# Transposing the gate by DMA in place of TensorE, and the second matmul issued in parts

## The chip, the cores and the metric

One core of one Trainium2 chip runs the program. The metric is the device time of one execution in microseconds; the time before is the median of five runs. A core has five engines that run side by side: TensorE (PE; its weight loads are listed as PEld), VectorE (DVE), ScalarE (ACT), GpSimd (POOL) and SyncE (SP). DMA transfers are issued by POOL and SP here, each in its own order.

## The reference

```python
def _attn_ref(u, v, z):                 # u, v: (8, 3008, 256), z: (8, 3008, 64), float32
    scores = (1.0 / S) * np.matmul(z, z.transpose(0, 2, 1))      # S = 3008
    attn = np.maximum(scores, 0.0) ** 2
    out = np.matmul(attn, v)
    return u * out

def _moe_ref(x, w_in, w_out):           # w_in: (256, 2048), w_out: (2048, 256)
    h = x @ w_in
    g = h * (1.0 / (1.0 + np.exp(-1.702 * h)))
    return g @ w_out

x = _attn_ref(u, v, z).reshape(24064, 256)
result = _moe_ref(x, w_in, w_out)       # (24064, 256) float32
```

## The kernel before

The 8 batches have 3008 tokens each, cut into 6 blocks: five of 512 and one of 448, so there are 48 blocks. Everything is kept transposed: features or keys stand on the partitions, tokens of the block in the free dimension.

`attention` (L207) makes one block. For each pair of 128-key tiles TensorE makes two score tiles (L217, `sc`, from `zT` on both sides), ScalarE takes the Relu (L227, `r`), VectorE squares it (L228, `at`), and three pairs later TensorE adds the pair into two accumulators (L258, `outps`, four matmuls for a pair). At the end VectorE multiplies the accumulators by the transposed gate `uT` into `xT` (L267).

`emit_phaseB` (L153) runs in front of the next block's attention. For each of the 16 slices of the hidden width it makes `hps` (L164, two matmuls), the sigmoid on ScalarE (L172, `sig`) and the product on VectorE (L180, `g`). Between these go the matmuls of the block before that one: `emit_ygroup` (L125) sums 16 matmuls of 256 columns (L130, `yps`) for each 128 tokens, and VectorE scales the sum out (L137, `ysb`). Group 0 comes first, groups 1 and 2 after slices 5 and 10, group 3 in the attention that follows.

`uT` comes from `dma_u` (L94), which brings the block of `u` to SBUF in float32 on SP's queue, and `emit_utr` (L117): TensorE transposes each 128x128 piece in float32 against an identity (L122, `ups`) and ScalarE copies it to `uT` (L123). There are 8 such pieces in a block, and those of the next block are handed to `emit_phaseB` as `tr_jobs`. `zT` comes another way: `dma_z` (L71) casts z to float16 in flight on POOL's queue into `z_st`, whose padding VectorE zeroes (L78, L80), and `emit_ztr` (L112) transposes 24 pieces of 128x128 with one DMA on SP's queue (L113). `load_v` (L83, issued at L85) and `load_weights` (L67) are casting loads on POOL's queue.

PSUM is cut in two pools: `ps_big` has three buffers, for `sc` and `hps`; `ps_small` has two, which `outps`, `yps` and `ups` share. The tiles `uT`, `u_st`, `z_st`, `vh` and `zT` have two buffers each.

A planner fixes the order of each engine's instructions when the program is built, from the order of the program, modelled durations and the buffers that are free. It may move an instruction ahead of others of its engine, so `yps` matmuls stand between `hps` matmuls in the trace where the program has them later. What it fixed is then carried out strictly in that order on each engine.

Of the kernel before, what the change touches and what calls it, by code (L numbers as in the profile page):

```python
# [8 lines left out]

FP32 = mybir.dt.float32  # L10
FP16 = mybir.dt.float16
AF = mybir.ActivationFunctionType
ALU = mybir.AluOpType


def cdiv(a, b):
    return (a + b - 1) // b
# [3 lines left out]
def kernel(  # L21
# [9 lines left out]
    nc = tc.nc  # L31
    P = 128

    B, S, D = u.shape
    dqk = z.shape[2]
    d_ff = moe_w_in.shape[1]
    ND = D // P
# [9 lines left out]

    inv_S2 = 1.0 / (float(S) * float(S))

    const = ctx.enter_context(tc.tile_pool(name="const", bufs=1))  # L50
    wpool = ctx.enter_context(tc.tile_pool(name="wpool", bufs=1))
    zvpool = ctx.enter_context(tc.tile_pool(name="zvpool", bufs=2))
    stage = ctx.enter_context(tc.tile_pool(name="stage", bufs=2))
# [4 lines left out]
    ps_big = ctx.enter_context(tc.tile_pool(name="ps_big", bufs=3, space=bass.MemoryType.PSUM))  # L58
    ps_small = ctx.enter_context(tc.tile_pool(name="ps_small", bufs=2, space=bass.MemoryType.PSUM))

    identf = const.tile([P, P], FP32, name="identf")
    make_identity(nc, identf)

    w_inh = wpool.tile([P, ND, d_ff], FP16, name="w_inh")
    w_outh = wpool.tile([P, NF, D], FP16, name="w_outh")

    def load_weights():  # L67
        nc.gpsimd.dma_start(w_inh, moe_w_in.rearrange("(h p) f -> p h f", p=P))
        nc.gpsimd.dma_start(w_outh, moe_w_out.rearrange("(f p) d -> p f d", p=P))

    def dma_z(b):  # L71
        z_st = zvpool.tile([P, NJ, P], FP16, name=f"z_st{b}", tag="z_st")
        nc.gpsimd.dma_start(  # L73
            z_st[:, : NJ - 1, :dqk],
            z[b, : (NJ - 1) * P, :].rearrange("(n p) m -> p n m", p=P),
        )
        nc.gpsimd.dma_start(z_st[:JL, NJ - 1, :dqk], z[b, (NJ - 1) * P :, :])
        nc.vector.memset(z_st[:, :, dqk:], 0.0)  # L78
        if JL < P:
            nc.vector.memset(z_st[JL:, NJ - 1, :dqk], 0.0)  # L80
        return z_st

    def load_v(b):  # L83
        vh = zvpool.tile([P, NJ, D], FP16, name=f"vh{b}", tag="vh")
        nc.gpsimd.dma_start(  # L85
            vh[:, : NJ - 1, :],
            v[b, : (NJ - 1) * P, :].rearrange("(n p) m -> p n m", p=P),
        )
        nc.gpsimd.dma_start(vh[:JL, NJ - 1, :], v[b, (NJ - 1) * P :, :])
        if JL < P:  # L90
            nc.vector.memset(vh[JL:, NJ - 1, :], 0.0)
        return vh

    def dma_u(b, blk):  # L94
        i0, ilen = blocks[blk]
        u_st = stage.tile([P, 4, D], FP32, name=f"ust_{b}_{blk}", tag="u_st")
        fullm = ilen // P
        if fullm:
            nc.sync.dma_start(
                u_st[:, :fullm, :],  # L100
                u[b, i0 : i0 + fullm * P, :].rearrange("(n p) m -> p n m", p=P),
            )
        if ilen % P:
            nc.sync.dma_start(
                u_st[: ilen % P, fullm, :], u[b, i0 + fullm * P : i0 + ilen, :]
            )
        return u_st

    def alloc_zT(b):
        return zvpool.tile([P, SP], FP16, name=f"zT{b}", tag="zT")  # L110

# [2 lines left out]
            zT.rearrange("p (n t) -> p n t", t=P), z_st[:, :, :]  # L114
        )

    def emit_utr(b, blk, uT, u_st, idx):  # L117
        i0, ilen = blocks[blk]
        m, h = divmod(idx, ND)
        ml = min(P, ilen - m * P)  # L120
        ups = ps_small.tile([P, P], FP32, name=f"ups_{b}_{blk}_{idx}", tag="pssmall")
        nc.tensor.transpose(ups[:, :ml], u_st[:ml, m, h * P : (h + 1) * P], identf[:ml, :ml])  # L122
        nc.scalar.copy(uT[:, h, m * P : m * P + ml], ups[:, :ml])  # L123

    def emit_ygroup(pend_y, m):  # L125
        gts_y, ilen_y, tok0_y, y_sb = pend_y
        ml = min(P, ilen_y - m * P)
        yps = ps_small.tile([P, IBS], FP32, name=f"yps_{tok0_y}_{m}", tag="pssmall")
        for ff in range(NF):
            nc.tensor.matmul(  # L130
                yps[:ml, :D],
                gts_y[ff][:, m * P : m * P + ml],
                w_outh[:, ff, :],
                start=(ff == 0),
                stop=(ff == NF - 1),
            )
        nc.vector.tensor_scalar_mul(y_sb[:ml, m, :], yps[:ml, :D], inv_S2)  # L137

    def emit_ydma(pend_y):
        gts_y, ilen_y, tok0_y, y_sb = pend_y  # L140
        full = ilen_y // P
        if full:
            nc.sync.dma_start(
                out[tok0_y : tok0_y + full * P, :].rearrange("(n p) d -> p n d", p=P),
                y_sb[:, :full, :],
            )
        if ilen_y % P:
            nc.sync.dma_start(
                out[tok0_y + full * P : tok0_y + ilen_y, :],
                y_sb[: ilen_y % P, full, :],  # L150
            )

    def emit_phaseB(pend_h, pend_y, tr_jobs, full_y):  # L153
        if pend_y is not None:
            emit_ygroup(pend_y, 0)
        new_pend = None
        if pend_h is not None:
            xT, ilen, tok0 = pend_h
            y_sb = work.tile([P, 4, D], FP32, name=f"ysb_{tok0}", tag="ysb")
            gts = []  # L160
            for f in range(NF):
                hps = ps_big.tile([P, IBS], FP32, name=f"hps_{tok0}_{f}", tag="psbig")
                for h in range(ND):
                    nc.tensor.matmul(  # L164
                        hps[:, :ilen],
                        w_inh[:, h, f * P : (f + 1) * P],
                        xT[:, h, :ilen],
                        start=(h == 0),
                        stop=(h == ND - 1),
                    )  # L170
                sig = sigp.tile([P, IBS], FP16, name=f"sig_{tok0}_{f}", tag="sig")
                nc.scalar.activation(  # L172
                    out=sig[:, :ilen],
                    in_=hps[:, :ilen],
                    func=AF.Sigmoid,
                    bias=0.0,
                    scale=1.702 * inv_S2,
                )
                gt = gpool.tile([P, IBS], FP16, name=f"g_{tok0}_{f}", tag=f"g{f}")
                nc.vector.tensor_tensor(gt[:, :ilen], hps[:, :ilen], sig[:, :ilen], ALU.mult)  # L180
                gts.append(gt)
                if pend_y is not None:
                    nsub_y = cdiv(pend_y[1], P)
                    if f == 5 and nsub_y > 1:
                        emit_ygroup(pend_y, 1)
                    elif f == 10 and nsub_y > 2:
                        emit_ygroup(pend_y, 2)
                ti = f // 2
                if f % 2 == 1 and ti < len(tr_jobs):
                    tr_jobs[ti]()  # L190
            for job in tr_jobs[NF // 2 :]:
                job()
            new_pend = [gts, ilen, tok0, y_sb]
        else:
            if pend_y is not None:
                for m in range(1, cdiv(pend_y[1], P)):
                    emit_ygroup(pend_y, m)
            for job in tr_jobs:
                job()
        if pend_y is not None and full_y:  # L200
            nsub_y = cdiv(pend_y[1], P)
            if pend_h is not None and nsub_y > 3:
                emit_ygroup(pend_y, 3)
            emit_ydma(pend_y)
        return new_pend

    def attention(b, blk, zT, vh, uT, pend_y):  # L207
# [57 lines left out]
        xT = work.tile([P, ND, IBS], FP16, name=f"xT_{b}_{blk}", tag="xT")  # L265
        for h in range(ND):
            nc.vector.tensor_tensor(  # L267
                xT[:, h, :ilen], outps[h][:, :ilen], uT[:, h, :ilen], ALU.mult
            )
        return xT  # L270

# [1 line left out]
    vh_cur = load_v(0)  # L273
    zT_cur = alloc_zT(0)
    emit_ztr(zT_cur, z_st_cur)
    u_st = dma_u(0, 0)
    load_weights()
    uT = stage.tile([P, ND, IBS], FP32, name="uT_0_0", tag="uT")
    for i in range(2 * cdiv(blocks[0][1], P)):
        emit_utr(0, 0, uT, u_st, i)  # L280

    z_st_next = vh_next = zT_next = None
    pend_h = None
# [2 lines left out]
    for b in range(B):  # L286
        zT = zT_cur
        vh = vh_cur
        for blk, (i0, ilen) in enumerate(blocks):
# [1 line left out]
                z_st_next = dma_z(b + 1)  # L291
                vh_next = load_v(b + 1)
            nxt = (b, blk + 1) if blk + 1 < NBLK else (b + 1, 0)
            tr_jobs = []
            uT_next = None
            if nxt[0] < B:
                u_st_n = dma_u(*nxt)
                uT_next = stage.tile(
                    [P, ND, IBS], FP32, name=f"uT_{nxt[0]}_{nxt[1]}", tag="uT"
                )  # L300
                nsub_n = cdiv(blocks[nxt[1]][1], P)
                for i in range(2 * nsub_n):
                    tr_jobs.append(
                        (lambda i=i, a=nxt[0], c=nxt[1], t=uT_next, s=u_st_n:
                         emit_utr(a, c, t, s, i))
                    )
            if b + 1 < B and blk == 1:
                zT_next = alloc_zT(b + 1)
                emit_ztr(zT_next, z_st_next)
            new_pend = emit_phaseB(pend_h, pend_y, tr_jobs, full_y=False)  # L310
            old_pend_y = pend_y
            pend_y = new_pend
            xT = attention(b, blk, zT, vh, uT, old_pend_y)
# [1 line left out]
            uT = uT_next  # L315
        zT_cur = zT_next
        vh_cur = vh_next
    pend_y2 = emit_phaseB(pend_h, pend_y, [], full_y=True)
    emit_phaseB(None, pend_y2, [], full_y=True)


# [28 lines left out]
```

## Time and profile before

| | |
|---|---|
| median of 5 runs | 1592.23 us (1589.49 to 1596.23) |
| profiled execution, its own time | 1594.62 us |
| its span, first to last instruction | 1592.9 us |
| mean granted TensorE clock | 0.998 of full speed |
| TensorE busy | 1484.8 us, 8448 matmuls |
| VectorE busy / ScalarE busy | 1034.0 us / 1046.4 us |
| DMA | 74.49 MB |

Busy time counts an instruction from its start to its modelled end. TensorE overlaps the end of one matmul with the start of the next, so the sum of durations is more than the time that they take up; distances between starts tell that time.

### The profile page before, as it was taken

The numbers are of one execution on the slowest core, as the hardware profiler recorded it, in microseconds if no ns is written. First come the engines' busy times: TensorE is split into PE (matmuls) and PEld (weight loads), VectorE is DVE, ScalarE is ACT, GpSimd is POOL, SyncE is SP. The second block draws the span as 40 slices with busy tenths as digits, with TensorE's granted clock in tenths as the row PEclk, the third lists the DMA queues.
The fourth block names the chain that finished last, engine by engine and source line by source line (L and its number), as shares of the span: only waits on it lengthen the run. The fifth ranks groups of instructions, "written<-read, shape, count | busy, mean of one in ns | idle before, by whom it ended". The sixth has DMA issues, their size and how long they took to land.

```text
span 1592.9 us, 22055 instructions
## 1 busy us (share of the span) xinstructions
PE 1484.8 (93%) x8448; PEld 836.3 (53%) x8448; DVE 1034.0 (65%) x1752; ACT 1046.4 (66%) x1826; POOL 35.6 (2%) x40
## 2 busy tenths in 40 slices
PE   1799999999999999999999999999999999999998
PEld 0255555555555555555555555555555555555555
DVE  0466676666766666666666666666676666766676
ACT  1576667766766767576756676667666766776665
POOL 2100010000100001000010000000000000000000
PEclk9999999999999999999999999999999999999999
DMA  9900061000700016001160111311032000110001
GB/s 147 128 25 27 27 96 51 26 27 27 122 26 25 28 43 106 26 26 41 40 95 26 39 40 47 66 37 40 27 73 63 27 27 27 40 39 26 14 14 39
DMA packets 125834, 74.49 MB, mean 47 GB/s; under 512 B 51232, under 2 KB 125472, under 8 KB 125728
## 3 DMA queue, kind: packets, MB, share of 16 engines
q1 hardware_dynamic: 74752, 55.58, 12.8%
q0 software_dynamic: 50976, 17.50, 10.2%
q8 instruction: 66, 1.08, 0.3%
q14 instruction: 40, 0.33, 0.1%
HBM read 59.64 MB, written 24.64 MB: 53 GB/s over the span
## 4 chain that ended last, share of the span: by engine, by line
PE 83%; ACT 6%; DVE 6%; DMA 4%; issue 1%; POOL 0%; DVEq 0%; POOLq 0%; SPq 0%
PE outps L258 29%; PE yps L130 23%; PE sc L217 15%; PE hps L164 15%; ACT sig L172 5%; DMA zT<-z_st 4%; DVE g L180 3%; DVE xT L267 2%; ACT uT L123 1%; DVE ysb L137 1%; PE ups L122 1%; DMA z_st<-in_z_dram 0%; DVE z_st L78 0%; POOL z_st L73 0%; ACT L172 0%
## 5 line engine op out<-in xcount | busy, mean ns | idle before, releaser
L172 ACT ACTIVATE sig<-hps 128x512 f16<-128x512 f32 (+1 forms) x768 | 434.7, 593 | 351.4 <-PE hps L164 295.5
L258 PE MATMUL outps<-at,vh 128*128 128x512 f16 (+1 forms) x2304 | 559.0, 375 | 7.9 <-DVE at L228 7.9
L180 DVE TENSOR_TENSOR g<-hps,sig 128x512 f16<-128x512 f32 (+1 forms) x768 | 486.6, 676 | 121.5 <-ACT sig L172 113.3
L227 ACT ACTIVATE r<-sc 128x1024 f16<-128x1024 f32 x480 | 474.3, 1028 | 121.2 <-PE sc L217 118.5
L228 DVE TENSOR_TENSOR at<-r 128x1024 f16<-128x1024 f16 x480 | 332.3, 692 | 257.5 <-ACT r L227 257.5
L130 PE MATMUL yps<-w_outh,g 128*128 128x256 f16 (+1 forms) x3072 | 419.9, 272 | 47.7 <-DVE xT L267 26.3
L164 PE MATMUL hps<-xT,w_inh 128*128 128x512 f16 (+1 forms) x1536 | 414.3, 375 | 13.2 <-DVE g L180 12.2
L130 PEld LDWEIGHTS <-g 128*128 128x128 f16 (+1 forms) x3072 | 300.4, 98 | 190.1 <-issue 90.3
L258 PEld LDWEIGHTS <-vh 128*128 128x128 f16 x2304 | 225.7, 98 | 270.9 <-issue 10.2
L217 PE MATMUL sc<-zT 128*128 128x512 f16 (+1 forms) x1152 | 323.7, 376 | 29.1 <-DMA zT<-z_st 28.9
L164 PEld LDWEIGHTS <-w_inh 128*128 128x128 f16 x1536 | 149.3, 98 | 94.4 <-issue 30.3
L217 PEld LDWEIGHTS <-zT 128*128 128x128 f16 x1152 | 111.7, 98 | 147.6 <-DMA zT<-z_st 29.2
L123 ACT COPY uT<-ups 128x128 f32<-128x128 f32 (+1 forms) x384 | 100.8, 282 | 51.0 <-PE ups L122 51.0
L137 DVE TENSOR_SCALAR ysb<-yps 128x256 f32<-128x256 f32 x192 | 80.5, 419 | 68.3 <-PE yps L130 66.8
L267 DVE TENSOR_TENSOR xT<-outps,uT 128x512 f16<-128x512 f32 (+1 forms) x96 | 60.8, 675 | 70.9 <-PE outps L258 70.9
L122 PE MATMUL ups<-identf,ust 128*128 128x128 f32 (+1 forms) x384 | 98.5, 281 | 6.4 <-DMA ust<-in_u_dram 4.6
L231 ACT ACTIVATE r<-sc 128x448 f16<-128x448 f32 x192 | 89.3, 568 | 10.9 <-PE sc L217 10.9
L236 DVE TENSOR_TENSOR at<-r 128x448 f16<-128x448 f16 x192 | 74.6, 392 | 20.0 <-ACT r L231 13.6
L122 PEld LDWEIGHTS ups<-identf,ust 128*128 128x128 f32 (+1 forms) x384 | 54.0, 142 | 49.4 <-issue 8.3
L85 POOL DMA_DIRECT2D vh<-in_v_dram x8 | 12.1, 1508 | 1099.6 <-PE outps L258 1099.6
L78 DVE MEMSET z_st<- 128x768 uint32 x8 | 5.6, 698 | 16.2 <-DMA zT<-z_st 14.9
L73 POOL DMA_DIRECT2D z_st<-in_z_dram x8 | 12.1, 1514 | 52.2 <-DMA zT<-z_st 50.9
(14 smaller groups left out, 16.7 us busy)
## 6 DMA issues: line engine op xcount, KB each, us to landing
ust<-in_u_dram SPq DMA_DIRECT2D x40, 512.0 KB, 3.9
out_dram<-ysb SPq DMA_DIRECT2D x40, 512.0 KB, 2.9
vh<-in_v_dram POOLq DMA_DIRECT2D x8, 1472.0 KB, 12.8
ust<-in_u_dram SPq DMA_DIRECT2D x8, 384.0 KB, 3.3
out_dram<-ysb SPq DMA_DIRECT2D x8, 384.0 KB, 2.6
z_st<-in_z_dram POOLq DMA_DIRECT2D x8, 368.0 KB, 12.8
w_inh<-in_moe_w_in_dram POOLq DMA_DIRECT2D x1, 1024.0 KB, 29.6
w_outh<-in_moe_w_out_dram POOLq DMA_DIRECT2D x1, 1024.0 KB, 39.3
```

The lines of the kernel that those rows point to most:

```text
L122: nc.tensor.transpose(ups[:, :ml], u_st[:ml, m, h * P : (h + 1) * P], identf[:ml, :ml])
L123: nc.scalar.copy(uT[:, h, m * P : m * P + ml], ups[:, :ml])
L130: nc.tensor.matmul(yps[:ml, :D], gts_y[ff][:, m * P : m * P + ml], w_outh[:, ff, :], start=(ff == 0), stop=(ff == NF - 1),)
L137: nc.vector.tensor_scalar_mul(y_sb[:ml, m, :], yps[:ml, :D], inv_S2)
L164: nc.tensor.matmul(hps[:, :ilen], w_inh[:, h, f * P : (f + 1) * P], xT[:, h, :ilen], start=(h == 0), stop=(h == ND - 1),)
L172: nc.scalar.activation(out=sig[:, :ilen], in_=hps[:, :ilen], func=AF.Sigmoid, bias=0.0, scale=1.702 * inv_S2,)
L180: nc.vector.tensor_tensor(gt[:, :ilen], hps[:, :ilen], sig[:, :ilen], ALU.mult)
L217: nc.tensor.matmul(scp[:, t * IBS : t * IBS + ilen], zT[:, jt * P : (jt + 1) * P], zT[:, i0 : i0 + ilen], start=True, stop=True,)
L227: nc.scalar.activation(out=rp[:, :, :], in_=scp[:, :], func=AF.Relu)
L228: nc.vector.tensor_tensor(atp[:], rp[:], rp[:], ALU.mult)
L258: nc.tensor.matmul(outps[h][:, :ilen], vh[:, jt, h * P : (h + 1) * P], atp[:, t, :ilen], start=(jt == 0), stop=(jt == NJ - 1),)
L267: nc.vector.tensor_tensor(xT[:, h, :ilen], outps[h][:, :ilen], uT[:, h, :ilen], ALU.mult)
```

## The change

The float32 transposes of u on TensorE, their copies on ScalarE, the identity and `tr_jobs` go. `load_uT` takes their place: up to four casting loads on POOL's queue bring the block of u to SBUF as float16, and two DMA transposes on SP's queue (one for each half of the features) write `uT`, now float16. In the block of 448 tokens GpSimd zeroes the staging tile first.

`gate` writes one element of a tile on GpSimd from the first `zT`, so that the loads into that tile start only after that transpose has landed: the weights, the first u, and the second batch's z and v. The zeroing of the padding of z moves from VectorE to GpSimd from the third batch on.

`emit_ygroup` can now be emitted in parts and from another pool: group 0 uses `ps_big`, and groups 1 and 2 are spread in sixths behind slices 0 to 5 and 6 to 11.

```diff
--- before.py
+++ after.py
...
-    identf = const.tile([P, P], FP32, name="identf")
-    make_identity(nc, identf)
-
     w_inh = wpool.tile([P, ND, d_ff], FP16, name="w_inh")
     w_outh = wpool.tile([P, NF, D], FP16, name="w_outh")
 
+    zT_first = []
+
+    def gate(ap):
+        # holds the loads into a tile back until the first z transpose has landed
+        nc.gpsimd.tensor_copy(ap, zT_first[0][:1, :1])
+
     def load_weights():
+        gate(w_inh[:1, 0, :1])
+        gate(w_outh[:1, 0, :1])
         nc.gpsimd.dma_start(w_inh, moe_w_in.rearrange("(h p) f -> p h f", p=P))
         nc.gpsimd.dma_start(w_outh, moe_w_out.rearrange("(f p) d -> p f d", p=P))
 
     def dma_z(b):
         z_st = zvpool.tile([P, NJ, P], FP16, name=f"z_st{b}", tag="z_st")
+        if b == 1:
+            gate(z_st[:1, 0, :1])
         nc.gpsimd.dma_start(
             z_st[:, : NJ - 1, :dqk],
             z[b, : (NJ - 1) * P, :].rearrange("(n p) m -> p n m", p=P),
         )
         nc.gpsimd.dma_start(z_st[:JL, NJ - 1, :dqk], z[b, (NJ - 1) * P :, :])
-        nc.vector.memset(z_st[:, :, dqk:], 0.0)
+        eng = nc.vector if b < 2 else nc.gpsimd
+        eng.memset(z_st[:, :, dqk:], 0.0)
         if JL < P:
-            nc.vector.memset(z_st[JL:, NJ - 1, :dqk], 0.0)
+            eng.memset(z_st[JL:, NJ - 1, :dqk], 0.0)
         return z_st
 
     def load_v(b):
         vh = zvpool.tile([P, NJ, D], FP16, name=f"vh{b}", tag="vh")
+        if b == 1:
+            gate(vh[:1, 0, :1])
         nc.gpsimd.dma_start(
             vh[:, : NJ - 1, :],
             v[b, : (NJ - 1) * P, :].rearrange("(n p) m -> p n m", p=P),
@@ -91,21 +99,6 @@
             nc.vector.memset(vh[JL:, NJ - 1, :], 0.0)
         return vh
 
-    def dma_u(b, blk):
-        i0, ilen = blocks[blk]
-        u_st = stage.tile([P, 4, D], FP32, name=f"ust_{b}_{blk}", tag="u_st")
-        fullm = ilen // P
-        if fullm:
-            nc.sync.dma_start(
-                u_st[:, :fullm, :],
-                u[b, i0 : i0 + fullm * P, :].rearrange("(n p) m -> p n m", p=P),
-            )
-        if ilen % P:
-            nc.sync.dma_start(
-                u_st[: ilen % P, fullm, :], u[b, i0 + fullm * P : i0 + ilen, :]
-            )
-        return u_st
-
     def alloc_zT(b):
         return zvpool.tile([P, SP], FP16, name=f"zT{b}", tag="zT")
 
@@ -114,19 +107,36 @@
             zT.rearrange("p (n t) -> p n t", t=P), z_st[:, :, :]
         )
 
-    def emit_utr(b, blk, uT, u_st, idx):
+    def load_uT(b, blk):
         i0, ilen = blocks[blk]
-        m, h = divmod(idx, ND)
-        ml = min(P, ilen - m * P)
-        ups = ps_small.tile([P, P], FP32, name=f"ups_{b}_{blk}_{idx}", tag="pssmall")
-        nc.tensor.transpose(ups[:, :ml], u_st[:ml, m, h * P : (h + 1) * P], identf[:ml, :ml])
-        nc.scalar.copy(uT[:, h, m * P : m * P + ml], ups[:, :ml])
-
-    def emit_ygroup(pend_y, m):
-        gts_y, ilen_y, tok0_y, y_sb = pend_y
+        nsub = cdiv(ilen, P)
+        u_st = stage.tile([P, ND, 4, P], FP16, name=f"ust_{b}_{blk}", tag="u_st")
+        if ilen < 4 * P:
+            nc.gpsimd.memset(u_st[:, :, :, :], 0.0)
+        for m in range(nsub):
+            ml = min(P, ilen - m * P)
+            if b == 0 and blk == 0:
+                gate(u_st[:1, 0, m, :1])
+            nc.gpsimd.dma_start(
+                u_st[:ml, :, m, :],
+                u[b, i0 + m * P : i0 + m * P + ml, :].rearrange("t (h dd) -> t h dd", h=ND),
+            )
+        uT = stage.tile([P, ND, 4, P], FP16, name=f"uT_{b}_{blk}", tag="uT")
+        for h in range(ND):
+            nc.sync.dma_start_transpose(uT[:, h], u_st[:, h])
+        return uT
+
+    def emit_ygroup(pend_y, m, parts=1, part=0, pool=ps_small, tag="pssmall"):
+        gts_y, ilen_y, tok0_y, y_sb = pend_y[:4]
         ml = min(P, ilen_y - m * P)
-        yps = ps_small.tile([P, IBS], FP32, name=f"yps_{tok0_y}_{m}", tag="pssmall")
-        for ff in range(NF):
+        if part == 0:
+            yps = pool.tile([P, IBS], FP32, name=f"yps_{tok0_y}_{m}", tag=tag)
+            pend_y[4] = yps
+        else:
+            yps = pend_y[4]
+        lo = NF * part // parts
+        hi = NF * (part + 1) // parts
+        for ff in range(lo, hi):
             nc.tensor.matmul(
                 yps[:ml, :D],
                 gts_y[ff][:, m * P : m * P + ml],
@@ -134,10 +144,11 @@
                 start=(ff == 0),
                 stop=(ff == NF - 1),
             )
-        nc.vector.tensor_scalar_mul(y_sb[:ml, m, :], yps[:ml, :D], inv_S2)
+        if hi == NF:
+            nc.vector.tensor_scalar_mul(y_sb[:ml, m, :], yps[:ml, :D], inv_S2)
 
     def emit_ydma(pend_y):
-        gts_y, ilen_y, tok0_y, y_sb = pend_y
+        gts_y, ilen_y, tok0_y, y_sb = pend_y[:4]
         full = ilen_y // P
         if full:
             nc.sync.dma_start(
@@ -150,10 +161,11 @@
                 y_sb[: ilen_y % P, full, :],
             )
 
-    def emit_phaseB(pend_h, pend_y, tr_jobs, full_y):
+    def emit_phaseB(pend_h, pend_y, full_y):
+        nsub_y = cdiv(pend_y[1], P) if pend_y is not None else 0
+        new_pend = None
         if pend_y is not None:
-            emit_ygroup(pend_y, 0)
-        new_pend = None
+            emit_ygroup(pend_y, 0, pool=ps_big, tag="psbig")
         if pend_h is not None:
             xT, ilen, tok0 = pend_h
             y_sb = work.tile([P, 4, D], FP32, name=f"ysb_{tok0}", tag="ysb")
@@ -179,27 +191,16 @@
                 gt = gpool.tile([P, IBS], FP16, name=f"g_{tok0}_{f}", tag=f"g{f}")
                 nc.vector.tensor_tensor(gt[:, :ilen], hps[:, :ilen], sig[:, :ilen], ALU.mult)
                 gts.append(gt)
-                if pend_y is not None:
-                    nsub_y = cdiv(pend_y[1], P)
-                    if f == 5 and nsub_y > 1:
-                        emit_ygroup(pend_y, 1)
-                    elif f == 10 and nsub_y > 2:
-                        emit_ygroup(pend_y, 2)
-                ti = f // 2
-                if f % 2 == 1 and ti < len(tr_jobs):
-                    tr_jobs[ti]()
-            for job in tr_jobs[NF // 2 :]:
-                job()
-            new_pend = [gts, ilen, tok0, y_sb]
+                m = 1 + f // 6
+                if pend_y is not None and m < min(nsub_y, 3):
+                    emit_ygroup(pend_y, m, parts=6, part=f % 6)
+            new_pend = [gts, ilen, tok0, y_sb, None]
         else:
             if pend_y is not None:
-                for m in range(1, cdiv(pend_y[1], P)):
+                for m in range(1, min(nsub_y, 3)):
                     emit_ygroup(pend_y, m)
-            for job in tr_jobs:
-                job()
         if pend_y is not None and full_y:
-            nsub_y = cdiv(pend_y[1], P)
-            if pend_h is not None and nsub_y > 3:
+            if nsub_y > 3:
                 emit_ygroup(pend_y, 3)
             emit_ydma(pend_y)
         return new_pend
@@ -265,7 +266,10 @@
         xT = work.tile([P, ND, IBS], FP16, name=f"xT_{b}_{blk}", tag="xT")
         for h in range(ND):
             nc.vector.tensor_tensor(
-                xT[:, h, :ilen], outps[h][:, :ilen], uT[:, h, :ilen], ALU.mult
+                xT[:, h, :ilen],
+                outps[h][:, :ilen],
+                uT[:, h].rearrange("p a b -> p (a b)")[:, :ilen],
+                ALU.mult,
             )
         return xT
 
@@ -273,11 +277,9 @@
     vh_cur = load_v(0)
     zT_cur = alloc_zT(0)
     emit_ztr(zT_cur, z_st_cur)
-    u_st = dma_u(0, 0)
+    zT_first.append(zT_cur)
+    uT = load_uT(0, 0)
     load_weights()
-    uT = stage.tile([P, ND, IBS], FP32, name="uT_0_0", tag="uT")
-    for i in range(2 * cdiv(blocks[0][1], P)):
-        emit_utr(0, 0, uT, u_st, i)
 
     z_st_next = vh_next = zT_next = None
     pend_h = None
@@ -291,23 +293,11 @@
                 z_st_next = dma_z(b + 1)
                 vh_next = load_v(b + 1)
             nxt = (b, blk + 1) if blk + 1 < NBLK else (b + 1, 0)
-            tr_jobs = []
-            uT_next = None
-            if nxt[0] < B:
-                u_st_n = dma_u(*nxt)
-                uT_next = stage.tile(
-                    [P, ND, IBS], FP32, name=f"uT_{nxt[0]}_{nxt[1]}", tag="uT"
-                )
-                nsub_n = cdiv(blocks[nxt[1]][1], P)
-                for i in range(2 * nsub_n):
-                    tr_jobs.append(
-                        (lambda i=i, a=nxt[0], c=nxt[1], t=uT_next, s=u_st_n:
-                         emit_utr(a, c, t, s, i))
-                    )
+            uT_next = load_uT(*nxt) if nxt[0] < B else None
             if b + 1 < B and blk == 1:
                 zT_next = alloc_zT(b + 1)
                 emit_ztr(zT_next, z_st_next)
-            new_pend = emit_phaseB(pend_h, pend_y, tr_jobs, full_y=False)
+            new_pend = emit_phaseB(pend_h, pend_y, full_y=False)
             old_pend_y = pend_y
             pend_y = new_pend
             xT = attention(b, blk, zT, vh, uT, old_pend_y)
@@ -315,8 +305,8 @@
             uT = uT_next
         zT_cur = zT_next
         vh_cur = vh_next
-    pend_y2 = emit_phaseB(pend_h, pend_y, [], full_y=True)
-    emit_phaseB(None, pend_y2, [], full_y=True)
+    pend_y2 = emit_phaseB(pend_h, pend_y, full_y=True)
+    emit_phaseB(None, pend_y2, full_y=True)
 
 
 # ---- launch: one core; inputs and outputs as the reference has them ----
```

## Rows read from the trace of the kernel before

**Rows 1.** The page, busy time and share of the span of each engine.
```profile
PE 1484.8 (93%) x8448; PEld 836.3 (53%) x8448; DVE 1034.0 (65%) x1752; ACT 1046.4 (66%) x1826; POOL 35.6 (2%) x40
```

**Rows 2.** The page, chain that ended last: shares by engine.
```profile
PE 83%; ACT 6%; DVE 6%; DMA 4%; issue 1%; POOL 0%; DVEq 0%; POOLq 0%; SPq 0%
```

**Rows 3.** Stretch of one batch: length, busy us per engine, clock, DMA share, GB/s.
```profile
417.06:609.40 192.34, 184.66 (x1056) 104.24 (x1056) 129.14 (x220) 130.25 (x228) 4.12 (x5) 1.00 0.22 47
```

**Rows 4.** Groups by line and shape: busy us, mean ns, idle before.
```profile
L123 ACT COPY uT<-ups 128x128 f32<-128x128 f32 x368 | 98.0, 283 | 51.0 <-PE ups L122 51.0
...
L122 PE MATMUL ups<-identf,ust 128*128 128x128 f32 x368 | 95.8, 282 | 6.4 <-DMA ust<-in_u_dram 4.6 <-DVE ysb L137 0.5
```

**Rows 5.** TensorE in time, block with transposes: start us, us, line, idle before.
```profile
1503.15 3.62 PE L258 MATMUL outps<-at,vh 128*128 128x512 f16 x16
1507.33 1.91 PE L130 MATMUL yps<-w_outh,g 128*128 128x256 f16 x16 [0.56 <-DVE xT L267]
...
1509.94 0.27 PE L122 MATMUL ups<-identf,ust 128*128 128x128 f32 x1
1510.05 0.59 PE L164 MATMUL hps<-xT,w_inh 128*128 128x512 f16 x2
1510.48 0.27 PE L122 MATMUL ups<-identf,ust 128*128 128x128 f32 x1
1511.00 0.38 PE L130 MATMUL yps<-w_outh,g 128*128 128x256 f16 x2 [0.25 <-ACT uT L123]
...
1523.82 1.46 PE L217 MATMUL sc<-zT 128*128 128x512 f16 x6
```

**Rows 6.** TensorE in time, the next block, which has no transposes.
```profile
1539.66 1.91 PE L130 MATMUL yps<-w_outh,g 128*128 128x256 f16 x16 [0.57 <-DVE xT L267]
1541.40 1.46 PE L164 MATMUL hps<-xT,w_inh 128*128 128x512 f16 x6
1542.70 0.71 PE L130 MATMUL yps<-w_outh,g 128*128 128x256 f16 x5
1543.41 0.59 PE L164 MATMUL hps<-xT,w_inh 128*128 128x512 f16 x2
...
1554.41 1.30 PE L217 MATMUL sc<-zT 128*128 128x448 f16 x6
```

**Rows 7.** VectorE in time, the same block.
```profile
1542.66 4.00 DVE L180 TENSOR_TENSOR g<-hps,sig 128x512 f16<-128x512 f32 x6 [0.64 <-ACT sig L172]
```

**Rows 8.** TensorE in time, the first block.
```profile
40.00 3.59 PE L217 MATMUL sc<-zT 128*128 128x512 f16 x8 [28.90 <-DMA zT<-z_st]
...
64.84 1.86 PE L258 MATMUL outps<-at,vh 128*128 128x512 f16 x4 [7.87 <-DVE at L228]
```

**Rows 9.** VectorE in time, ends of the first two blocks.
```profile
66.32 1.29 DVE L267 TENSOR_TENSOR xT<-outps,uT 128x512 f16<-128x512 f32 x2 [1.38 <-PE outps L258]
...
96.52 1.29 DVE L267 TENSOR_TENSOR xT<-outps,uT 128x512 f16<-128x512 f32 x2 [1.49 <-PE outps L258]
```

**Rows 10.** Chain that ended last, first 80 us: start us, us, what.
```profile
8.72 31.23 DMA zT<-z_st
...
48.54 14.70 DMA zT<-z_st
...
63.55 0.70 DVE z_st L78
```

**Rows 11.** The tile zT: its eight DMA transposes, issue to landing.
```profile
DMA to landing us min/median/max: 5.5/5.5/31.2
```

**Rows 12.** Waits: who for whom, us in total, times, longest.
```profile
POOL vh L85 <- PE outps L258: 1099.6, 6, 189.7
...
PE yps L130 <- ACT uT L123: 21.4, 86, 0.2
```

**Rows 13.** The page, DMA issues: count, KB each, median us to landing.
```profile
vh<-in_v_dram POOLq DMA_DIRECT2D x8, 1472.0 KB, 12.8
...
w_inh<-in_moe_w_in_dram POOLq DMA_DIRECT2D x1, 1024.0 KB, 29.6
```

More of the change, by code (lines that the diff above doesn't have):

```diff
@@ L6 @@
 from concourse import bass_utils, mybir
-from concourse.masks import make_identity
 from concourse._compat import with_exitstack
@@ L48 @@
     inv_S2 = 1.0 / (float(S) * float(S))
-    const = ctx.enter_context(tc.tile_pool(name="const", bufs=1))
     wpool = ctx.enter_context(tc.tile_pool(name="wpool", bufs=1))
```

## The prediction

> **What bounds the kernel now.** I read the busy times first, then the chain that ended last, then one batch as a stretch, then TensorE instruction by instruction in two neighbouring blocks. TensorE is busy 93% of the span [rows 1] and carries 83% of the chain [rows 2], so it is the engine to look at; a batch repeats every 192.34 us at full granted clock [rows 3]. VectorE and ScalarE are busy 129 and 130 us of it and are not the bound over a batch, but both can be inside `emit_phaseB`, which has little TensorE work for each `g`. DMA share is 0.22 of a batch: there is room for more transfers.
>
> Busy time misleads about the transposes. 368 of them are listed at 282 ns, 95.8 us [rows 4], but a transpose at 1509.94 is followed by the next matmul at 1510.05 [rows 5]: its slot is 0.11 us, as the ends overlap. What it costs beside the slot is a wait. A `yps` matmul behind the next transpose starts 0.52 us after it, not 0.11, because the `ps_small` buffer that it takes is still being copied by ScalarE (283 ns a copy [rows 4]); the waits list shows this 86 times, and its 21.4 us count only what exceeds the modelled ends [rows 12].
>
> The trace holds the experiment already. The block that starts its second phase at 1539.66 has no next `uT` to make, since it precedes the last one. From the first `yps` to the six-fold `sc` its predecessor, with transposes, takes 1523.82 - 1507.33 = 16.49 us [rows 5]; it takes 1554.41 - 1539.66 = 14.75 us [rows 6]. Two score matmuls in the second stretch have 448 columns for 512 (about 0.05 us). So the eight transposes cost 16.49 - 14.75 - 0.05 = **1.69 us a block**, 0.88 of it slots (8 x 0.11) and the rest waits.
>
> **The change part by part.** *Transposes and copies go.* They lie in the second phase of 46 blocks (not the first, whose transposes run while TensorE has nothing else, and not the last two): 46 x 1.69 = 77.7 us. ScalarE's 98 us of copies lie beside TensorE and are worth nothing beyond the waits already in 1.69.
>
> *Group 0 moves to `ps_big`.* Today it waits for VectorE to read both `outps` buffers: the 16 `outps` from 1503.15 take 16 x 0.216 = 3.46 us of slots (two `hps` take 0.43 from 1510.05 to 1510.48), so TensorE could go on at 1506.61 and goes on at 1507.33 [rows 5]. In `ps_big` the buffers were given up by Relu well before. The gap of 0.72 us goes, and group 0 (1541.40 - 1539.66 = 1.74 us [rows 6]) covers VectorE's two products (1.29 us [rows 9]) on which `hps` waits. It comes up 47 times: 47 x 0.72 = 33.8 us.
>
> *Groups 1 and 2 in sixths.* In the block without transposes one stall is left: five `yps` take 0.71 us to the next `hps` where five slots are 5 x 0.109 = 0.54 [rows 6], three times a block, 0.5 us. Spreading could remove all of it (46 x 0.5 = 23 us gained). Or it could hurt: with groups 1 and 2 used up by slice 11, the last four slices have two `hps` slots (0.43 us) against VectorE's pace for `g`, (4.00 - 0.69)/5 = 0.66 us [rows 7], 4 x 0.23 = 0.92 us a block and 43 us lost, if group 3 doesn't fill in. The planner puts group 3 between the last `hps` today, so I take a value near the gain's side: 7 us.
>
> *Loads and DMA transposes for u.* All of it lies beside TensorE. A block now needs eight 128x128 pieces transposed; 24 pieces of z take 5.5 us at the median from issue to landing, and 31.2 us in the one case where the queues were full [rows 11]. So eight take below 5.5, at worst a third of 31.2 = 10.4. The casting load is bounded above by the larger one of v, 12.8 us [rows 13]. Together at most 23 us. They are issued when the previous use of the tiles ends, about one block ahead: (192.34 - 6 x 2.4)/6 = 29.6 us. Covered, so the price is nothing. POOL's queue waits for a buffer of v up to 189.7 us [rows 12], and now u loads stand in that queue; but v's buffer comes free when the last attention of a batch ends, a whole block before the u behind it is multiplied, and a planner can't put an earlier-needed u behind it without a deadlock. GpSimd's zeroing and the gates are a few short instructions on an engine busy for 2% [rows 1].
>
> The Trainium skill speaks against this step: "VectorE: DVE Perf Modes", The three transpose paths and Rules for kernel authors, advises TensorE for a 128x128 transpose where PSUM will do, and prices the DMA way at 1309 ns, TensorE at 390. By that eight pieces would be an estimated 10.5 us, still under the cover, and the sum would stay; the trace has 5.5 us for 24 pieces, 229 ns each, so the row disagrees with the page's price here.
>
> *The start.* TensorE starts at 40.00, released by the first `zT`, which took 31.23 us from 8.72 beside v, the weights and the second batch's loads [rows 8, 10]. With the gates only v is beside it. Bounds for the landing: 8.72 + 5.5 = 14.2 if v costs nothing, 8.72 + 12.8 + 5.5 = 27.0 if all of v goes first. I take 21: 19 us earlier. In the first block TensorE also stands 7.87 us [rows 8] while VectorE has the zeroing L78 at the head of its queue, held by the second `zT` from 48.54 to 63.2 [rows 10]; that zeroing now sits on GpSimd: 8 us. Sum 27 us, bounds 34 and 21. What is late next: `uT` and the weights, now behind the gate. The first block's attention is 66.32 - 40.00 - 7.87 = 18.4 us [rows 8, 9], so both have until about 39; from 21, u and `w_in` (29.6 us with v, a larger load, ahead of it [rows 13]) fit barely. The second `uT` has until about 39 + 28 = 67 and stands behind the weights, z and v: a few us may be lost, within the bounds.
>
> The Trainium skill, "DMA: Bandwidth & Descriptors", Queues, rings and completion order, says each DMA engine takes turns between queues packet by packet. That would give the transposes half the engines and a landing near 8.7 + 2 x 5.5 = 19.7 us, 1.3 us off the sum; the 31.2 us in full queues [rows 11] is worse than a half, so the trace doesn't bear it out.
>
> **The sum**, against the profiled execution's own 1594.6 us: 1594.6 - 77.7 - 33.8 - 7 - 27 = 1449. The median of runs lies 2.4 us under that execution: **1447**. With the better ends (23, 34) it is 1424, with the worse (-43, 21) 1503.
>
> **Rivals.** *The start gives little.* Gates make weights and u late, and the 27 us are lost again: 1447 + 27 = 1474. For it: the same bytes pass in the same time. Against: they are needed only after 18 us of attention.
>
> *The second phase becomes VectorE's.* With TensorE pinned slice by slice to three `ps_big` buffers, it follows VectorE: from the end of `outps` two products and one pace more (1.29 + 0.66), 1.26 from the first `hps` to the first `g` [rows 6, 7], 16 x 0.66, three `ysb` of half the columns (by estimate half a pace each, 1.0), then group 3 uncovered, 1.74: 16.55 us against 16.49 + 0.72 = 17.21 today. That saves 0.66 x 46 = 30, with the start 57: 1535. Against: the block without transposes ran 14.75 on the same three buffers [rows 6].
>
> *Busy time is what counts.* 98 us of transposes at their listed length [rows 4], 33.8, 21.4 of waits [rows 12] and 27 go: 1592.2 - 180 = 1412. Against: the starts in [rows 5].
>
> *`uT` comes late (slower).* The place is the product at L267, which then holds `outps` and TensorE. It begins when load and transposes pass 29.6 us, and costs 47 us for each us beyond; the gain of 145 is used up at 29.6 + 3.1 = 32.7, and at 34 it is 1447 + 47 x 4.4 = 1654. For it: three queues in strict order (POOL's wait for v, SP's for `ysb`) and 31.2 us once [rows 11, 12]. Against: 23 us at the worst rows.
>
> **How the numbers follow.** Forecast 0.68, lost start 0.12, VectorE's phase 0.10, busy time 0.05, late `uT` 0.05. The first two lie in 1422 to 1500, which leaves out 2 in 10. About 0.3% is what a measurement of this kernel can tell from no change. Faster: 0.95; the late `uT` splits into slower 0.04 and same 0.01.
>
> **What the profile would show.** Right: no L122 and L123; TensorE's first `yps` of a block right behind `outps`; first score near 21 us; a batch from one load of v to the next in about 177 us (192.34 - 6 x 2.55); ScalarE near 950 us. Wrong: idle time of VectorE at the product with a DMA to `uT` as its end (late `uT`); `hps` released by `g` in every slice (VectorE's phase); the first `xT` later than 50 us (lost start).

## The result and the profile after

The changed kernel takes 1436.32 us (median of 8 runs, 1435.22 to 1437.51) against 1592.61 (median of 15): a ratio of 0.9019, 95% interval 0.9007 to 0.903. The forecast was 1447 us, in a range of 1422 to 1500. The profiled execution took 1436.37 us.

From the page of the changed kernel, the busy times and, further down, the shares of the chain that ended last:

```profile
PE 1407.9 (98%) x8064; PEld 785.2 (55%) x8064; DVE 1029.3 (72%) x1740; ACT 1012.8 (71%) x1442; POOL 186.1 (13%) x258
...
PE 98%; DMA 1%; DVE 0%; ACT 0%; POOL 0%; issue 0%; SPq 0%; POOLq 0%
```

TensorE has 384 matmuls fewer than in [rows 1], and the chain runs through it nearly alone (98%): ScalarE and VectorE, 6% each in [rows 2], are gone from it. One batch as a stretch (columns as in [rows 3]):

```profile
183.44:358.84 175.40, 175.40 (x1011) 98.07 (x1009) 128.45 (x218) 126.29 (x180) 23.25 (x32) 1.00 0.33 52
```

175.40 us against 192.34 [rows 3]; TensorE's busy time fills it to the last digit. TensorE in time, from one block to the next (columns as in [rows 5]):

```profile
764.84 3.62 PE L259 MATMUL outps<-at,vh 128*128 128x512 f16 x16
768.29 1.91 PE L140 MATMUL yps<-w_outh,g 128*128 128x256 f16 x16
770.04 0.59 PE L176 MATMUL hps<-xT,w_inh 128*128 128x512 f16 x2
770.47 0.38 PE L140 MATMUL yps<-w_outh,g 128*128 128x256 f16 x2
770.69 0.59 PE L176 MATMUL hps<-xT,w_inh 128*128 128x512 f16 x2
...
778.72 1.08 PE L176 MATMUL hps<-xT,w_inh 128*128 128x512 f16 x4
779.64 0.60 PE L140 MATMUL yps<-w_outh,g 128*128 128x256 f16 x4
780.13 0.59 PE L176 MATMUL hps<-xT,w_inh 128*128 128x512 f16 x2
780.56 0.38 PE L140 MATMUL yps<-w_outh,g 128*128 128x256 f16 x2
...
782.74 1.46 PE L218 MATMUL sc<-zT 128*128 128x512 f16 x6
...
797.84 1.91 PE L140 MATMUL yps<-w_outh,g 128*128 128x256 f16 x16
```

Sixteen `outps` at 0.216 us end at 768.30 and group 0 starts at 768.29: the gap of 0.72 us in [rows 5] is closed. Slices and sixths follow without idle time, where [rows 6] had five `yps` take 0.71 us. A block takes 797.84 - 768.29 = 29.55 us. A block has 104 matmuls of 512 columns and 64 of 256; their slots alone are 104 x 0.2157 + 64 x 0.109 = 29.41 us, so hardly any waiting is left to take out.

The start, in the chain of the first 45 us and in VectorE's products (columns as in [rows 10] and [rows 9]):

```profile
7.63 12.86 DMA zT<-z_st
20.53 3.60 PE sc L218 x8
```

```profile
38.58 1.29 DVE L268 TENSOR_TENSOR xT<-outps,uT 128x512 f16<-128x512 f32 x2 [1.49 <-PE outps L259]
66.69 1.29 DVE L268 TENSOR_TENSOR xT<-outps,uT 128x512 f16<-128x512 f32 x2 [1.49 <-PE outps L259]
96.24 1.29 DVE L268 TENSOR_TENSOR xT<-outps,uT 128x512 f16<-128x512 f32 x2 [1.49 <-PE outps L259]
```

The first product comes 66.32 - 38.58 = 27.7 us earlier than in [rows 9], the second 96.52 - 66.69 = 29.8.

### The profile page after: what moved, and what is told of

It is laid out like the page before. It is cut to its first block, busy times and chain, and to the rows that moved or that the text cites. A ratio compares the mean times of both kernels' runs of the same rounds, so it can differ in the third digit from the quotient of the medians.

```text
span 1434.6 us, 21391 instructions
## 1 busy us (share of the span) xinstructions
PE 1407.9 (98%) x8064; PEld 785.2 (55%) x8064; DVE 1029.3 (72%) x1740; ACT 1012.8 (71%) x1442; POOL 186.1 (13%) x258
## 4 chain that ended last, share of the span: by engine, by line
PE 98%; DMA 1%; DVE 0%; ACT 0%; POOL 0%; issue 0%; SPq 0%; POOLq 0%
PE outps L259 34%; PE yps L140 24%; PE hps L176 23%; PE sc L218 17%; DMA zT<-z_st 1%; DMA z_st<-in_z_dram 0%; DVE g L192 0%; ACT sig L184 0%; POOL z_st L78 0%; DVE xT L268 0%; DVE ysb L148 0%; SPq L106 0%; POOLq L324 0%
## 5 line engine op out<-in xcount | busy, mean ns | idle before, releaser
L184 ACT ACTIVATE sig<-hps 128x512 f16<-128x512 f32 (+1 forms) x768 | 446.5, 588 | 308.1 <-PE hps L176 296.5
L192 DVE TENSOR_TENSOR g<-hps,sig 128x512 f16<-128x512 f32 (+1 forms) x768 | 498.2, 677 | 52.1 <-ACT sig L184 33.5
L140 PE MATMUL yps<-w_outh,g 128*128 128x256 f16 (+1 forms) x3072 | 466.4, 273 | 0.0
L176 PE MATMUL hps<-xT,w_inh 128*128 128x512 f16 (+1 forms) x1536 | 444.3, 374 | 2.5 <-DVE g L192 1.8
L120 POOL DMA_DIRECT2D ust<-in_u_dram x192 | 133.5, 699 | 783.8 <-DMA uT<-ust 751.1
L115 POOL MEMSET ust<- 128x1024 f16 x8 | 7.6, 952 | 189.0 <-DMA uT<-ust 189.0
L78 POOL DMA_DIRECT2D z_st<-in_z_dram x8 | 12.1, 1508 | 12.1 <-DMA vh<-in_v_dram 10.4
L84 POOL MEMSET z_st<- 128x1536 f16 x6 | 8.4, 1393 | 0.0
L82 POOL DMA_DIRECT2D z_st<-in_z_dram x8 | 4.5, 563 | 0.0
```

The source lines that it names most:

```text
L120: nc.gpsimd.dma_start(u_st[:ml, :, m, :], u[b, i0 + m * P : i0 + m * P + ml, :].rearrange("t (h dd) -> t h dd", h=ND),)
L140: nc.tensor.matmul(yps[:ml, :D], gts_y[ff][:, m * P : m * P + ml], w_outh[:, ff, :], start=(ff == 0), stop=(ff == NF - 1),)
L176: nc.tensor.matmul(hps[:, :ilen], w_inh[:, h, f * P : (f + 1) * P], xT[:, h, :ilen], start=(h == 0), stop=(h == ND - 1),)
L184: nc.scalar.activation(out=sig[:, :ilen], in_=hps[:, :ilen], func=AF.Sigmoid, bias=0.0, scale=1.702 * inv_S2,)
```

## The experiments

Five kernels undo one part of the change each and keep the rest, and one makes only the DMA part on the kernel before; four more load the DMA or the start in other ways. I compare medians with the 1436.3 us of the changed kernel, and the distance between VectorE's products of two full blocks. Beside these runs the kernel before lay at 1589.87 to 1590.73 us and beside the changed kernel at 1592.61, so a difference of 2 or 3 us in the medians says nothing by itself.

VectorE in time, three products of the kernel before behind the two of [rows 9]:

```profile
128.90 1.29 DVE L267 TENSOR_TENSOR xT<-outps,uT 128x512 f16<-128x512 f32 x2 [1.49 <-PE outps L258]
161.28 1.29 DVE L267 TENSOR_TENSOR xT<-outps,uT 128x512 f16<-128x512 f32 x2 [1.49 <-PE outps L258]
193.60 1.29 DVE L267 TENSOR_TENSOR xT<-outps,uT 128x512 f16<-128x512 f32 x2 [1.49 <-PE outps L258]
```

A full block takes 32.38 us before, 32.32 where the next block has 448 tokens and so smaller transposes, and 29.55 after.

**Only the DMA transposes, on the kernel before.**

```diff
# the changed kernel without its other parts
-        nc.gpsimd.tensor_copy(ap, zT_first[0][:1, :1])
+        pass
...
-        eng = nc.vector if b < 2 else nc.gpsimd
+        eng = nc.vector
...
-            emit_ygroup(pend_y, 0, pool=ps_big, tag="psbig")
+            emit_ygroup(pend_y, 0)
...
# and groups 1 and 2 whole, after slices 5 and 10
```

> One part alone on the kernel before: uT by casting load and DMA transpose; no gate, zeroing on VectorE, group 0 in ps_small, groups 1 and 2 whole. Theory: 78 us off the kernel before (1592.6), 1515 us, with the first score again near 40 us and VectorE's zeroing again in the way. Rival: uT comes late or the start grows worse because u now stands in the same queue as the weights, and less than half of the 78 us shows: above 1554 us.

1512.38 us (ratio to before 0.9494, 0.9466 to 0.9522). VectorE in time, two products in the steady part:

```profile
121.96 1.29 DVE L270 TENSOR_TENSOR xT<-outps,uT 128x512 f16<-128x512 f32 x2 [1.49 <-PE outps L261]
152.61 1.29 DVE L270 TENSOR_TENSOR xT<-outps,uT 128x512 f16<-128x512 f32 x2 [1.49 <-PE outps L261]
```

30.65 us a block: 1.73 less than 32.38 and 1.67 less than 32.32, where the prediction had read 1.69 from one block of the second kind. Over the 45 blocks behind the second product it is 1.70 on the mean: 1592.9 - 96.52 = 1496.4 us of the span are left there before, 1420.0 here. The rival's late `uT` does not appear; each product waits only for `outps`.

**TensorE's transposes back, the rest kept.**

```diff
-            uT_next = load_uT(*nxt) if nxt[0] < B else None
+            # dma_u on SP and tr_jobs of emit_utr, as in the kernel before
```

> Undoes the transposes alone: u comes by SP in float32 and is transposed by TensorE and copied by ScalarE, as before; gates, zeroing, the pool of group 0 and the sixths stay. Theory, the term as predicted: 46 x 1.69 = 78 us, 1514 us. Rival 1: the waits for the copies were a matter of whole groups in ps_small and don't come back, only the slots of 0.11 us do: 46 x 0.88 = 40 us, 1477 us. Rival 2, busy time counts: 98 us and the waits of 21, 1556 us.

1495.11 us, 58.8 more than the changed kernel: between the two theories. A block takes 30.85 us, 1.30 more than 29.55. TensorE in time, in two places of the same block:

```profile
134.33 0.27 PE L135 MATMUL ups<-identf,ust 128*128 128x128 f32 x1
134.44 0.59 PE L185 MATMUL hps<-xT,w_inh 128*128 128x512 f16 x2
...
137.59 0.59 PE L185 MATMUL hps<-xT,w_inh 128*128 128x512 f16 x2
138.16 0.38 PE L149 MATMUL yps<-w_outh,g 128*128 128x256 f16 x2
```

The slot of 0.11 us is there again. The `yps` right behind the second transpose of a pair in [rows 5], which cost 0.4 us each time, are not: sixths of a group stand elsewhere. What waits there are, are short (0.57 us from `hps` to `yps` for two slots of 0.43). So 0.88 of the 1.30 us is slots, and the other 0.42 I put down to waits like this one; with whole groups it was 0.88 and 0.82. How much the transposes cost depends on what stands behind them.

**Group 0 back in `ps_small`.**

```diff
-            emit_ygroup(pend_y, 0, pool=ps_big, tag="psbig")
+            emit_ygroup(pend_y, 0)
```

> Undoes the pool of group 0 alone: it takes a ps_small buffer again, the rest is the changed kernel. Theory: TensorE waits again for VectorE's two products in front of every block, 47 x 0.72 = 34 us, 1470 us. Rival: the wait only changes its place, since the hps matmuls need the same products; then group 0 in ps_small costs nothing and the time stays at 1436.

1471.0 us, 34.7 more, as the theory has it; a block takes 30.28 us. The wait is the old one, 47 times (waits list; total, times, longest):

```profile
PE yps L140 <- DVE xT L268: 26.3, 47, 0.6
```

**Groups 1 and 2 whole.**

```diff
-                m = 1 + f // 6
-                if pend_y is not None and m < min(nsub_y, 3):
-                    emit_ygroup(pend_y, m, parts=6, part=f % 6)
+                if pend_y is not None:
+                    if f == 5 and nsub_y > 1:
+                        emit_ygroup(pend_y, 1)
+                    elif f == 10 and nsub_y > 2:
+                        emit_ygroup(pend_y, 2)
```

> Undoes the sixths alone: groups 1 and 2 are emitted whole after slices 5 and 10, as in the kernel before; the rest is the changed kernel (1436.3). Theory: the stalls of 0.5 us a block that the block without transposes showed come back, three a block of about 0.17 us, so 46 x 0.5 = 23 us, 1459 us. If the prediction's term of 7 us was right: 1443. Rival: the planner fills the same gaps whatever the order of the program, 1436.

1453.39 us, 17.1 more; a block takes 29.92 us, 0.37 more. TensorE in time:

```profile
630.46 1.46 PE L176 MATMUL hps<-xT,w_inh 128*128 128x512 f16 x6
631.75 0.71 PE L140 MATMUL yps<-w_outh,g 128*128 128x256 f16 x5
632.46 0.59 PE L176 MATMUL hps<-xT,w_inh 128*128 128x512 f16 x2
```

This is the pattern of [rows 6], three times a block, five `yps` in 0.71 us. The stall over the slots is 29.92 - 29.41 = 0.51 us, as read; the sixths leave 0.14 of it, so they bring 0.37 and not 0.5, and much more than the 7 us in the sum.

**No gates.**

```diff
-        nc.gpsimd.tensor_copy(ap, zT_first[0][:1, :1])
+        pass
```

> Undoes the gates alone: weights, the first u and the second z and v are loaded at once, beside the first zT. Theory: the first score is near 40 us again instead of 20.5, 19 us lost, 1455 us. Rival: what the gate wins at the start is lost again later because weights and u come late; without it the time stays at 1436 although the first score moves.

1451.41 us, 15.1 more. TensorE's first instruction:

```profile
35.90 3.59 PE L218 MATMUL sc<-zT 128*128 128x512 f16 x8 [35.90 <-DMA zT<-z_st]
```

The first score moves from 20.53 to 35.90, 15.4 us, and all of it arrives in the end: the rival, a gain lost again later, falls.

**The zeroing back on VectorE.**

```diff
-        eng = nc.vector if b < 2 else nc.gpsimd
+        eng = nc.vector
```

> Undoes the move of the zeroing alone: VectorE zeroes the padding of z in all batches. Theory: in the first block or the one after it TensorE stands again while VectorE's queue is held by the second zT, 8 us or more lost, 1444 us or more. Rival: with the gate the second z and its transpose come later than VectorE's place for it, and the wait is longer than 8 us (up to 20, 1456). Rival 2: the wait falls where TensorE has other work, 1436.

1462.95 us, 26.6 more (the profiled execution, 1459.70, is the shortest of four). VectorE in time, the first two blocks:

```profile
38.06 1.29 DVE L268 TENSOR_TENSOR xT<-outps,uT 128x512 f16<-128x512 f32 x2 [1.49 <-PE outps L259]
58.34 0.70 DVE L84 MEMSET z_st<- 128x768 uint32 x1 [19.00 <-DMA ust<-in_u_dram]
58.96 1.82 DVE L192 TENSOR_TENSOR g<-hps,sig 128x512 f16<-128x512 f32 x3
```

The first product is not late (38.06), but behind it VectorE stands for 19 us in front of the zeroing; the second product comes at 85.19 instead of 66.69, 18.5 us later, over twice the 7.87 us of [rows 8]. By the code this zeroing, the padding of the fourth batch, writes the buffer that the second `zT` reads. That transpose, as SP issues it, and the time to its landing:

```profile
42.90 8.93 SPq L106 DMA_TRANSPOSE zT<-z_st  x1
DMA to landing us min/median/max: 15.1/15.1/15.1
```

It ends at 58.0, just ahead of the zeroing at 58.34. The release inferred names a load of u that ends next to it (58.2), but by the code the zeroing has no need of that load. The same zeroing without gates, in the kernel with only the DMA transposes:

```profile
63.82 0.70 DVE L84 MEMSET z_st<- 128x768 uint32 x1 [6.41 <-DMA zT<-z_st]
```

There the second `zT` is issued at 48.50 and the wait is 6.41 us. So the gate does not make that transpose late. It brings VectorE to the zeroing 18 us earlier (39.35 against 57.41, the ends of the first products), and the transpose comes only 5.6 earlier: gate and move belong together. Of the batches that follow, the next four lose 2.3, 0.6, 0.7 and 0.6 us, the last three nothing.

**Each DMA transpose issued four and fourteen times.**

```diff
-        for h in range(ND):
-            nc.sync.dma_start_transpose(uT[:, h], u_st[:, h])
+        for _ in range(4):                      # 14 in the second kernel
+            for h in range(ND):
+                nc.sync.dma_start_transpose(uT[:, h], u_st[:, h])
```

> Each DMA transpose of u is issued four times, eight in a block in place of two. Theory, uT is covered by about a block of other work: eight take 10 to 20 us and end before the product that needs them, 1436 us. Rival (DMA time counts, or the transfers disturb the engines): some 7.5 us more a block, 1790 us.

> Each DMA transpose of u is issued fourteen times, 28 in a block. Theory: 28 x 1.25 us = 35 us of issue alone exceed the 29.6 us of a block, so uT comes late and each block takes as long as its transposes: at least 48 x 35 = 1680 us, and VectorE's product waits for the DMA to uT. Rival: the cover is longer than one block and the time stays.

Four times: 1455.72 us, 19.4 more, so the expectation of 1436 was missed. VectorE in time, the first two products:

```profile
56.94 1.29 DVE L269 TENSOR_TENSOR xT<-outps,uT 128x512 f16<-128x512 f32 x2 [19.28 <-DMA uT<-ust]
86.57 1.29 DVE L269 TENSOR_TENSOR xT<-outps,uT 128x512 f16<-128x512 f32 x2 [1.49 <-PE outps L260]
```

The loss arises by the second product: 56.94 against 38.58 is 18.4 us, 86.57 against 66.69 is 19.9. The first block's transposes run beside the other loads of the start, where SP issues the eight in 27.35 us (from 27.68 on), and no earlier block covers them. From there on a block takes 29.55 us again, and a batch 175.4. In the steady part eight transposes, 10.4 us of issue from 117.44 on, are covered; the rival's 7.5 us a block does not appear.

Fourteen times: 2142.32 us (one execution). VectorE in time, three blocks, and SP's issue of one set:

```profile
653.18 0.69 DVE L269 TENSOR_TENSOR xT<-outps,uT 128x512 f16<-128x512 f32 x1 [4.28 <-DMA uT<-ust]
654.47 0.69 DVE L269 TENSOR_TENSOR xT<-outps,uT 128x512 f16<-128x512 f32 x1 [0.60 <-DMA uT<-ust]
694.99 0.69 DVE L269 TENSOR_TENSOR xT<-outps,uT 128x512 f16<-128x512 f32 x1 [12.02 <-DMA uT<-ust]
...
737.50 0.69 DVE L269 TENSOR_TENSOR xT<-outps,uT 128x512 f16<-128x512 f32 x1 [12.91 <-DMA uT<-ust]
```

```profile
676.71 38.86 SPq L127 DMA_TRANSPOSE uT<-ust  x28
```

Now the DMA ends the wait at 85 of the 96 products, and a block takes 694.99 - 653.18 = 41.8 or 42.5 us, more than the 35 expected; SP needs 38.9 us for the 28 alone. This is what the late `uT` of the prediction looks like. From 300 to 900 us TensorE is busy 424.7 of 600 us, so it idles some 12 us a block, and its granted clock is 0.84 on the mean there, against 1.00 in the changed kernel, which has no such gaps.

**Two tries at an earlier start.**

```diff
# v of the first batch, after emit_ztr(zT_cur, z_st_cur)
+        cuts = [0, 4, 8, 14, NJ - 1] if b == 0 else [0, NJ - 1]
+        for c0, c1 in zip(cuts, cuts[1:]):
+            if b == 0:                          # second kernel: and c0 > 0
+                gate(vh[:1, c0, :1])
             nc.gpsimd.dma_start(vh[:, c0:c1, :], ...)
# second kernel: the first zT in three transposes of 8 tiles, the gate on the last
```

> The changed kernel with the first v behind the gate too, in four pieces, so that the first z transpose runs with nothing beside it. Theory (the transpose took 12.9 us instead of 5.5 because v's load was beside it): first score near 13 us instead of 20.5, and the first pieces of v land before the first attention needs them; 5 to 7 us less, 1430 us. Rival: v is now what the first attention waits for, and the gain at the first score is lost before the first product at 38.6 us; 1436 or more.

> As the run before, but the first z transpose is cut into three of eight tiles each, and the first four tiles of v are not gated; the gate opens with the last third. Theory: the first score comes after one third of the transposes, near 10.5 us, and the first product some 9 us earlier than in the changed kernel; 1427 us. Rival: v's piece beside the first third slows it and v's other pieces are late; no better than the run before.

1435.21 us (1434.45 to 1435.39) and 1436.31 us: at best 1.1 less than the changed kernel, whose runs these ranges touch. In the first of them, the transpose in the chain, TensorE and then VectorE in time:

```profile
7.40 5.58 DMA zT<-z_st
```

```profile
13.03 3.25 PE L222 MATMUL sc<-zT 128*128 128x512 f16 x8 [13.03 <-DMA zT<-z_st]
18.87 1.57 PE L263 MATMUL outps<-at,vh 128*128 128x512 f16 x4 [2.60 <-DMA vh<-in_v_dram]
```

```profile
36.00 0.69 DVE L272 TENSOR_TENSOR xT<-outps,uT 128x512 f16<-128x512 f32 x1 [3.14 <-DMA uT<-ust]
38.19 0.69 DVE L272 TENSOR_TENSOR xT<-outps,uT 128x512 f16<-128x512 f32 x1 [1.50 <-DMA uT<-ust]
```

The first score is 7.5 us earlier, since the transpose alone takes 5.6 us instead of 12.9. Then TensorE waits 2.6 us for v, and the product waits for `uT`, whose load now stands behind v's: its second half ends at 38.19 + 0.69 = 38.88, against 38.58 + 1.29 = 39.87 in the changed kernel. In the second kernel the first score comes at 10.85, as expected, TensorE then waits 4.5 us for v, and the second half starts at 38.10. In both orders the first product waits for the DMA and gains about 1 us at most, so the rival holds; another order was not tried.

## Why the prediction was right

**The transposes: 1.69 us a block, 77.7 us.** Right. Alone on the kernel before they gave 1.70 us a block on the mean. The listed 282 ns was the trap: with the slot of 0.11 us and the waits, the block without transposes gave the price to a few hundredths of a us. That the medians beside each other differ by 77.5 us too (1589.87 - 1512.38) is in part luck: their ratio is known to 4.5 us either way, and in the profiled execution 5.2 us come from the start (second product at 91.32 against 96.52). The price holds for whole groups; with sixths, putting the transposes back cost 58.8, as the waits behind them are half as long.

**Group 0: 33.8 us.** Right: 34.7 when undone.

**The sixths: 7 us.** The right mechanism, mis-sized: 17.1. The step that failed is the choice between its ends "near the gain's side", which took under a third of the 23 us and feared VectorE's pace in slices 12 to 15. Group 3 fills those slices: `yps` stand at 779.64 and 780.56 between their `hps`, without idle time.

**The start: 27 us.** Right to the first product: 27.7. The first score was put at 21 and came at 20.53, 19.5 us earlier, and the attention behind it takes 18.05 us instead of 26.32, 8.3 less: the split of 19 and 8. As prices of single parts these figures don't hold: the gate gave 15.1 when undone, as without it the first score came at 35.9 and no longer at 40 (why is not shown), and the zeroing gave 26.6, as the gate lengthens its wait. The two overlap, and their single prices don't add up to the start's gain.

**`uT` covered, price nothing.** Right: eight transposes a block change nothing in the steady part, 28 make nearly every block wait. GpSimd is busy 13% instead of 2%, 133.5 us of it the issue of the 192 loads of u, and no row shows TensorE waiting for it in the steady part.

The sum closes in the periods: 32.38 or 32.32 to 30.65 (transposes, 1.70 on the mean), 30.65 to 29.92 (group 0; the gates and the zeroing, added in the same step, act at the start and by at most 2.3 us a batch), 29.92 to 29.55 (sixths). In us: 45 x 1.70 + 47 x 0.73 + 46 x 0.37 = 127.8 beyond the second product, and 29.8 before it, make 157.6 against 1592.9 - 1434.6 = 158.3 in the spans. The prediction's parts add up to 145.5; the 12.8 us more are the sixths' 10 and the start's 2.8 by the second product, and the small rest cancels. In the medians 11 us are left, between 1447 and 1436: the forecast took off 2.4 us because the profiled execution before was slower than the median, and the one after is not.

One sign named ahead was wrong: ScalarE's busy time was to be near 950 us and is 1012.8. Before, the busy times of ScalarE's groups add up to 1101.7 us, 55 more than the page's 1046.4, so instructions overlap there; afterwards they add up to 1012.7 and nothing overlaps. So taking 101 us of copies away took only 34 us of busy time.

**The rivals.** Busy time as the measure (1412) falls with the slots seen in both kernels and with the transposes put back: 1495 us, where it asked for 1556. VectorE's phase (1535) falls: from the first `yps` to the six-fold `sc` it is 782.74 - 768.29 = 14.45 us and not 16.55, as `g` keeps up when TensorE has 0.72 us of work a slice; it does bind in the one phase without `yps`, the first, where the changed kernel's `hps` wait for `g`. The lost start (1474) falls with the first product at 38.58 and the gates' experiment. The late `uT` is real, but needs far more than the two DMA transposes of a block: with eight it does not show in the steady part.

## What to carry to other kernels

Look for a stretch of the trace in which the thing to be removed is already missing, such as the first or last round of a loop: it prices slots and waits together, which no sum of durations does. Price a part that orders work by the stalls that it can remove, each looked up in the trace, and ask whether something else already fills the place where it could lose. When a change brings an engine's work forward, list every instruction in its strict order that waits for a transfer which does not come forward with it; the same wait cost over twice as much here afterwards (18.5 us against 7.87).

## What was not expected of the hardware

The same 24-piece DMA transpose took 5.6 us alone, 12.9 us beside the load of v and 31.2 us beside all loads of the start [rows 11]; the two of four pieces ahead of a block took 2.5 us each from issue to landing at the median and 10.4 at most. In this kernel a transpose by DMA was cheap where nothing stood beside it, and its place in time set its price.
